# Sketched attention feeding a gated FFN: q by head in sixteen 32x32 tiles, numerators in column tiles, W without masks, wo in 2 KB rows, three products on GpSimd

## The chip, the cores and the metric

The kernel runs on one core of one Trainium2 chip. The metric is the device time of one execution in microseconds (us). The engines are TensorE (PE; its weight loads are listed apart as PEld), VectorE (DVE), ScalarE (ACT), GpSimd (POOL) and SyncE (SP), which here only issues transfers. Each engine works through its own queue in order.

## The reference, cut to what matters

There are 4 batches, 4 heads, 1088 tokens and 32 dimensions a head; the sketch rank r is 8. Then x, with 4352 rows of 128, goes through a gated FFN with 1536 hidden units.

```python
def phi(x):                       # 32 -> 64 features
    a = np.einsum('rd,bhsd->bhsr', S1, x)
    b = np.einsum('rd,bhsd->bhsr', S2, x)
    return np.einsum('bhsi,bhsj->bhsij', a, b).reshape(*x.shape[:-1], r * r)
q_p, k_p = phi(q), phi(k)
kv = np.einsum('bhsf,bhsd->bhfd', k_p, v)
z = np.sum(k_p, axis=2)
num = np.einsum('bhsf,bhfd->bhsd', q_p, kv)
den = np.einsum('bhsf,bhf->bhs', q_p, z)[..., None] + 1e-06
x = (num / den).transpose(0, 2, 1, 3).reshape(B * S, H * D)
out = (np.maximum(x @ w_gate, 0.0) * (x @ w_val)) @ w_out
```

## The kernel before, in words

The whole kernel is a list of tasks, each with an engine, an assumed cost, what it depends on and how many PSUM banks it needs. `Plan.run` (lines 86 to 198) turns the list into one static order: for each engine it takes, among the tasks that can start soonest, the one with the earliest due time (`due`, lines 57 to 84 for attention, `T0 + STEP * u` for FFN unit `u`). `find` (lines 100 to 119) gives a task its banks among seven of the eight; the eighth (`OB`) collects outputs. While attention tasks remain, FFN tasks may hold five banks (`f_max`) and attention three (`a_max`). The table `land` holds the times at which loads are assumed to land, and `at` keeps a task from being planned earlier. The order is fixed at build time; on the chip the engines wait for each other by semaphores.

**Keys** (lines 445 to 596), once per batch: k is loaded with head and 32 token groups on partitions and transposed in 32x32 blocks on DVE (`t1`, L453). Sixteen fp32 PE instructions (L465) multiply it with the masked sketch `sk` into two banks; DVE transposes the result back (`t2`, L482). `phi` (L344) makes the 64 features a token, `kv` (L574) sums features times v, `z` (L527) sums the features through the two sketches, `zd` (L538) masks z on DVE, `w` (L546) turns it into the vector W by which q gives the denominator, and `wst` (L554, DVE) stores W beside S1 and S2. `kvc` (L590, DVE) stores kv as a masked block diagonal.

**Queries** (lines 605 to 790) come in groups of 64-token blocks of two halves, so a group of n holds n x 128 tokens: batch 0 in groups of 1, 1, 2 and 4, batches 1 to 3 in groups of 8, and a last group of 2 for the remaining tokens of all batches. q stands with two heads and 64 tokens on partitions. `t1` (L651, L653, L656) transposes it on DVE, `ab` (L675, L680 for the last group) multiplies with S1, S2 and W of the batch in 64x64 tiles into two banks, with the weights of a head masked to its half; `t2` (L690) transposes back. `bw`, `dn`, `rd`, `an` (L700 to L717) make the denominator and divide the first sketch by it, and `phi` (L344) makes the features on POOL (on DVE for the first two groups). The features are transposed on PE (L734) or by DMA (L764, batches 1 to 3), `num` (L741) multiplies four blocks with kv in two full-width matmuls that accumulate, and ACT writes the result into `xT` (L783).

**FFN** (lines 793 to 901): 102 units of 512 products a partition. A unit is a gate matmul and a value matmul (L821) of 512 columns in all, each into its own bank; relu on ACT (L833); the product on DVE straight from PSUM (L842), after which the value bank is free; and four output matmuls (L853). A unit covers four blocks of 128 tokens for one slice of 128 hidden units (later groups) or one or two blocks for four or two slices (first groups).

**Loads**: SP loads S1, k and q of batch 0; POOL loads v of batch 0 with a cast (L275), then gate and value weights in three parts each, then wo (L409). `e_later` (L426) waits for the first weights to land by a small transfer that reads them (L427), then issues k of batch 1, waits for that in the same way (L429), then q and v of batch 1 and k and q of batch 2. The other loads come where the plan puts them on SP, as do the stores (L877, two a part of a group).

Filler matmuls on zeros (L917) are put into gaps of PE that the plan foresees before the first gate matmul: one for each 107 ns of a gap before `T_WARM`, one for each 57 ns of nine tenths of it later.

## Time and profile before

| | us |
|---|---|
| three executions | 105.01, 105.17, 106.96 (median 105.17) |
| the profiled execution | 105.96 |
| its span, first to last instruction | 104.0 |
| first gate matmul | 15.24 |
| q of batch 1 landed (first transpose of it) | 23.77 |
| first xT of batch 1 | 38.82 |
| last output copied out of PSUM | 100.46 to 100.75 |

The engine line gives busy time, share of the span and number of instructions. The slices cut the span in 40 parts of 2.6 us, with a digit for the busy tenths of each. A group line gives line, engine, operation, tiles and shapes, then the busy time, the mean ns of one, the idle time ahead, and what ended it. Means of matmuls are latencies of pipelined instructions; their cost in a dense stretch is read from the spacing of their starts.

### The profile page before, as it was taken

The page shows a single profiled execution, that of the slowest core. Times are in us where ns is not written, and L with a number is a line of the kernel's source. Part 1 is how long each engine was busy: PE and PEld are TensorE (multiplying, and loading weights), DVE is VectorE, ACT ScalarE, POOL GpSimd, SP SyncE. Part 2 cuts the span into 40 slices and gives each one's busy share as a digit, 9 for nine tenths or more (in the row PEclk, how much of TensorE's full clock was granted, in tenths as well). Part 3 has the DMA queues.
Part 4 walks back from the last instruction along what each step waited for, and adds up shares of the span by engine and source line. Part 5 has one row for each costly group of instructions (what it writes and reads, how often), then busy time and mean ns, then how long its engine had stood idle before and what let it go on. Part 6 is the DMA issues. An engine that isn't in the chain of part 4 may idle for free.

```text
span 104.0 us, 3090 instructions
## 1 busy us (share of the span) xinstructions
PE 98.2 (94%) x1166; PEld 66.5 (64%) x1166; DVE 91.2 (88%) x200; ACT 77.5 (74%) x156; POOL 48.4 (47%) x71
## 2 busy tenths in 40 slices
PE   5999999996999999999999999999999999999960
PEld 5847988785666655565575565655765666667950
DVE  2866677988999999999999999999997999899950
ACT  4457028869798838689997895899789969999930
POOL 6999716089929829530980970129700015000000
PEclk9999999999999999999999999999999999999997
DMA  1999899789402489997049104000673300130024
GB/s 18 292 225 169 183 217 116 239 209 324 144 2 54 83 145 129 298 338 181 3 87 199 23 0 104 0 0 0 59 176 75 92 18 0 26 75 0 6 48 106
DMA packets 15711, 11.60 MB, mean 111 GB/s; under 512 B 9040, under 2 KB 13392, under 8 KB 15696
## 3 DMA queue, kind: packets, MB, share of 16 engines
q1 hardware_dynamic: 12520, 9.87, 38.9%
q0 software_dynamic: 2992, 1.46, 10.8%
q8 instruction: 9, 0.15, 0.5%
q10 hardware_dynamic: 184, 0.07, 0.2%
q14 instruction: 6, 0.05, 0.2%
HBM read 9.05 MB, written 2.23 MB: 108 GB/s over the span
## 4 chain that ended last, share of the span: by engine, by line
PE 66%; DMA 16%; ACT 5%; POOL 4%; DVE 2%; SPq 1%; issue 1%; ACTq 0%; POOLq 0%
PE ps L821 37%; PE ps L853 19%; DMA q_sb<-in_q_dram 6%; DMA k_sb<-in_k_dram 5%; DMA wg<-in_moe_w_gate_dram 4%; ACT g_sb L833 3%; PE ps L675 3%; PE ps L741 3%; POOL v_sb L275 2%; PE ps L574 2%; PE ps L465 1%; DVE qt L653 1%; ACT xT L783 1%; SPq L427 1%; DVE ht L842 1%
## 5 line engine op out<-in xcount | busy, mean ns | idle before, releaser
L842 DVE TENSOR_TENSOR ht<-g_sb,ps 128x512 f16<-128x512 f16 x102 | 64.0, 674 | 2.9 <-ACT g_sb L833 2.2
L833 ACT ACTIVATE g_sb<-ps 128x512 f16<-128x512 f32 x102 | 58.2, 605 | 11.1 <-PE ps L821 8.6
L853 PEld LDWEIGHTS <-ht 128*128 128x128 f16 x408 | 29.3, 98 | 18.5 <-DVE ht L842 4.5
L853 PE MATMUL ps<-wo,ht 128*128 128x128 f16 x408 | 37.6, 219 | 0.9 <-ACT g_sb L833 0.9
L821 PE MATMUL ps<-xT,wv 128*128 128x512 f16 (+2 forms) x132 | 37.8, 331 | 0.0
L821 PE MATMUL ps<-xT,wg 128*128 128x512 f16 (+2 forms) x132 | 35.8, 330 | 0.3
L344 POOL TENSOR_TENSOR kp<-abk 128x512 f16<-128x512 f32 (+1 forms) x14 | 16.3, 1199 | 5.2 <-DVE abk L482 5.2
L344 POOL TENSOR_TENSOR qp<-an,abq 128x512 f16<-128x512 f32 x16 | 16.7, 1068 | 0.5
L821 PEld LDWEIGHTS <-wg 128*128 128x128 f16 x132 | 12.0, 97 | 3.6 <-issue 1.1
L700 POOL TENSOR_TENSOR bw<-abq 128x128 f32<-128x128 f32 (+1 forms) x9 | 3.8, 422 | 21.1 <-DVE abq L690 19.3
L821 PEld LDWEIGHTS <-wv 128*128 128x128 f16 x132 | 11.6, 98 | 2.6 <-issue 0.6
L917 PE MATMUL ps<-zero 128*128 128x128 f16 x75 | 8.8, 293 | 1.1 <-DVE maskkv L319 1.1
L717 POOL TENSOR_TENSOR an<-abq,rd 128x256 f32<-128x256 f32 (+2 forms) x6 | 2.9, 479 | 11.6 <-DVE rd L714 11.6
L917 PEld LDWEIGHTS <-zero 128*128 128x128 f16 x75 | 6.8, 134 | 1.4 <-DVE maskkv L319 1.1
L690 DVE STREAM_TRANSPOSE abq<-ps 128x512 f32<-128x512 f32 (+2 forms) x11 | 6.3, 583 | 0.6 <-PE ps L675 0.6
L783 ACT CAST xT<-ps 128x512 f16<-128x512 f32 (+2 forms) x11 | 5.4, 491 | 1.8 <-PE ps L741 1.7
L775 ACT COPY pt<-ps 128x256 f16<-128x256 f16 (+2 forms) x5 | 2.9, 584 | 4.7 <-PE ps L734 4.7
L870 ACT ACTIVATE o_st<-ps 128x512 f32<-128x512 f32 (+2 forms) x10 | 5.1, 515 | 0.9 <-PE ps L853 0.9
L453 DVE STREAM_TRANSPOSE kt<-k_sb 128x576 f32<-128x576 f32 (+1 forms) x8 | 5.5, 720 | 0.2 <-DMA k_sb<-in_k_dram 0.2
L675 PE MATMUL ps<-qt,wst 64*64 64x256 f32 (+3 forms) x112 | 5.5, 336 | 0.0
L741 PE MATMUL ps<-pt,kv_bd 128*128 128x512 f16 (+2 forms) x20 | 5.1, 336 | 0.0
L653 DVE STREAM_TRANSPOSE qt<-q_sb 128x512 f32<-128x512 f32 x6 | 4.1, 696 | 0.8 <-DMA q_sb<-in_q_dram 0.8
(76 smaller groups left out, 67.8 us busy)
## 6 DMA issues: line engine op xcount, KB each, us to landing
out_dram<-o_st SPq DMA_DIRECT2D x14, 128.0 KB, 2.5
k_sb<-in_k_dram SPq DMA_DIRECT2D x3, 544.0 KB, 4.2
q_sb<-in_q_dram SPq DMA_DIRECT2D x3, 544.0 KB, 5.9
v<-in_v_dram SPq DMA_DIRECT2D x9, 144.0 KB, 4.7
q_sb<-in_q_dram SPq DMA_DIRECT2D x3, 128.0 KB, 3.4
wg<-in_moe_w_gate_dram POOLq DMA_DIRECT2D x3, 128.0 KB, 4.8
wv<-in_moe_w_val_dram POOLq DMA_DIRECT2D x3, 128.0 KB, 4.9
wo<-in_moe_w_out_dram POOLq DMA_DIRECT2D x1, 384.0 KB, 7.3
```

What stands on the lines that cost most here:

```text
L344: eng.tensor_tensor(out=dst.rearrange("s x (i j) -> s x i j", i=R), in0=a[:, :, :, None].to_broadcast([128, n, R, R]), in1=b[:, :, None, : ...
L453: nc.vector.transpose(kt[b][:, lo:hi].rearrange("p c t -> p (c t)"), k_sb[b][:, lo * D:hi * D])
L653: nc.vector.transpose(G.qt[:, hp], src[:, hp, :, G.c0:G.c0 + G.n])
L675: nc.tensor.matmul(o, wst[G.bs[0]][r, hp].rearrange("p a f -> p (a f)"), G.qt[r, hp, st], start=True, stop=True, skip_group_check=True)
L690: nc.vector.transpose(G.ab[:, lo:hi].rearrange("p x h f -> p h x f"), ps[:, f.bank:f.bank + 2, lo * 32:hi * 32].rearrange("p h (x t) -> p ...
L741: nc.tensor.matmul(o, kv_bd[G.bs[0]][:, 2 * hp:2 * hp + 2].rearrange("f a d -> f (a d)"), G.ptc[:, hp, c0:c0 + n], start=hp == 0, stop=hp ...
L783: emit=lambda t, p=p, f=num: nc.scalar.copy(out=xT[:, p.col:p.col + p.n * 128], in_=ps[:, f.bank, 0:p.n * 128]))
L821: nc.tensor.matmul(ps[:, t.bank, y * W:(y + 1) * W], w[:, j], xT[:, p.col:p.col + W], start=True, stop=True)
L833: nc.scalar.activation(out=U.g_sb, in_=ps[:, g.bank], func=ACTF.Relu)
L842: nc.vector.tensor_tensor(out=U.ht, in0=U.g_sb, in1=ps[:, vv.bank], op=ALU.mult)
L853: nc.tensor.matmul(ps[:, ob() + s, 0:DM] if final else ps[:, OB, s * DM:(s + 1) * DM], U.ht[:, y * n * 128 + s * 128:y * n * 128 + (s + 1) ...
L917: nc.tensor.matmul(ps[:, OB, 0:128], zero, zero, start=True, stop=True)
```

## The change

- **q**: loaded like k, with head and 32 token groups on partitions. `ab` becomes sixteen matmuls, four heads by four token groups, each in a 32x32 tile, a head to a bank, so that it needs four neighbouring banks; the transpose back gives two banks free at a time. Batch 0 has two sketches (four blocks each) instead of four. The last group reuses the transposes of the others, so its own four go.
- **Numerators**: two heads to a 64-column tile, each with its own result rows, no accumulation and no zeros.
- **W**: `zd` and `wst` become plain copies on ACT, for the masks are not needed; S1 by head comes from one DVE transpose instead of a matmul with a selection. `kvc` moves to ACT for batches 1 to 3.
- **v of batch 0** is loaded by SP without a cast and cast on ACT. k and q have two buffers instead of four. Fills go to POOL, ahead of the weight loads.
- **Hidden units** are dealt so that wo comes in rows of 2 KB; the gate and value weights are then read with a step of four elements.
- **Units 1, 3 and 5** copy the value out of PSUM on ACT and multiply on POOL.
- **Stores** are one transfer a part. `NG` and `NH` grow from 10 and 14 to 12 and 16; `T_WARM` is 8000 instead of 5500, `STEP` 800 instead of 830, and some landing times differ.
- **Plan**: a task of four banks may exceed the attention limit by two, and while one waits, bank tasks that are due later are held back. Tasks on POOL keep to due times also after the first FFN unit.

```diff
+            most = self.n_banks
+            if t.kind == "f" and n_att:
+                most = self.f_max
+            elif t.kind != "f" and started_f:
+                most = self.a_max + 2 * (t.banks > 2)
...
+                    if started_f and t.banks and t.due > want:
+                        continue
...
-    load_q0(nc.sync, 0)
-    load_q0(nc.sync, 1)
+    load_q(nc.sync, 0, 0, 4 * Q0)
+    load_v(nc.sync, 0)
+    load_q(nc.sync, 0, 4 * Q0, KC)
...
+        nc.scalar.copy(out=wst[:, :, 0:2 * R],
+                       in_=ps[:, t_st.bank, None, 0:2 * R].to_broadcast([128, B, 2 * R]))
...
+        return w.rearrange("m (y f j) -> m y j f", y=3, j=JT)
...
+                emit=e_load(wo, moe_w_out.rearrange("(y f j) m -> f y (j m)", y=3, j=JT)))
...
+        K.zd = P.add(f"k{b}zd", "ACT", **act(32), deps=[x], emit=lambda t, b=b, z=K.z:
+                     nc.scalar.copy(out=zd[b], in_=ps[:, z.bank, 0:H * R]))
...
+            for h in range(H):
+                nc.tensor.matmul(ps[32 * h:32 * h + 32, z.bank, 64:64 + R], s1h[:, h],
+                                 zd[b][:, h * R:(h + 1) * R], start=True, stop=True)
...
+        def qe_ab(t, bs, c0, n):
+            for h in range(H):
+                r = slice(32 * h, 32 * h + 32)
+                for g in range(4):
...
+                    nc.tensor.matmul(
+                        ps[32 * g:32 * g + 32, t.bank + h, 0:n * 32], wst[r, b],
+                        qt[b][r, lo:lo + n].rearrange("p c t -> p (c t)"), start=True, stop=True,
+                        skip_group_check=True)
...
             for hp in range(2):
-                    nc.tensor.matmul(
-                        o, kv_bd[G.bs[0]][:, 2 * hp:2 * hp + 2].rearrange("f a d -> f (a d)"),
-                        G.ptc[:, hp, c0:c0 + n], start=hp == 0, stop=hp == 1)
+                o = ps[64 * hp:64 * hp + 64, t.bank, 0:n * 128]
+                for x, b in enumerate(G.bs):
+                    y = 128 // len(G.bs)
+                    nc.tensor.matmul(
+                        o.rearrange("f (c t) -> f c t", c=n)[:, :, x * y:(x + 1) * y], kv_bd[b][:, hp],
+                        G.ptc[:, hp, c0:c0 + n, x * y:(x + 1) * y], start=True, stop=True,
+                        skip_group_check=True)
...
+            def e_multp(t, U):
+                U.ht = f_h.tile([128, 512], FP16, name="ht")
+                nc.gpsimd.tensor_tensor(out=U.ht, in0=U.g_sb, in1=U.v_sb, op=ALU.mult)
+
+            on_pool = u in ON_POOL
...
-                n = int(max(gap - 100.0, 0.0) / 107.0) if now > 2000.0 else int(gap / 107.0)
+                n = int(max(gap + (0.0 if now < 2000.0 else 60.0), 0.0) / 107.0)
```

## The prediction, made before the changed kernel ran

> **What bounds the kernel now.** I read the page's engine line and slices first, then the windows view, then the groups of the long stretch, then the timeline of PE.
>
> ```profile
> PE 98.2 (94%) x1166; PEld 66.5 (64%) x1166; DVE 91.2 (88%) x200; ACT 77.5 (74%) x156; POOL 48.4 (47%) x71
> ...
> PE   5999999996999999999999999999999999999960
> ...
> DVE  2866677988999999999999999999997999899950
> ACT  4457028869798838689997895899789969999930
> ```
>
> PE and VectorE (DVE) both stand at nine tenths from the ninth slice on, so neither alone is the limit. The windows view puts numbers to it (columns: us, then busy us and count of PE, weight loads, DVE, ACT, POOL).
>
> ```profile
> 23.00:26.00 3.00, 2.11 (x29) 1.66 (x28) 2.23 (x5) 2.56 (x5) 3.00 (x4) 1.00 0.93 302
> 26.00:98.30 72.30, 72.06 (x785) 45.43 (x783) 70.15 (x131) 61.28 (x114) 30.04 (x34) 1.00 0.38 83
> ```
>
> DVE is busy 70.15 of 72.30 us. PE's 72.06 is a modelled figure, so I count its real work from the same stretch by the spacing of starts, not by the mean durations:
>
> ```profile
> L853 PE MATMUL ps<-wo,ht 128*128 128x128 f16 x350 | 33.3, 219 | 0.0
> L821 PE MATMUL ps<-xT,wv 128*128 128x512 f16 x84 | 31.0, 379 | 0.0
> L741 PE MATMUL ps<-pt,kv_bd 128*128 128x512 f16 x14 | 4.2, 379 | 0.0
> L675 PE MATMUL ps<-qt,wst 64*64 64x256 f32 x48 | 3.3, 389 | 0.0
> L680 PE MATMUL ps<-qt,wst 64*64 64x32 f32 x32 | 0.7, 223 | 0.0
> ```
>
> ```profile
> 37.97 0.38 PE L821 MATMUL ps<-xT,wv 128*128 128x512 f16 x1
> 38.19 0.59 PE L741 MATMUL ps<-pt,kv_bd 128*128 128x512 f16 x2
> 38.62 0.39 PE L853 MATMUL ps<-wo,ht 128*128 128x128 f16 x4
> ...
> 42.40 0.39 PE L853 MATMUL ps<-wo,ht 128*128 128x128 f16 x4
> 42.62 0.38 PE L821 MATMUL ps<-xT,wv 128*128 128x512 f16 x1
> 42.93 1.09 PE L675 MATMUL ps<-qt,wst 64*64 64x256 f32 x16
> 43.96 0.39 PE L821 MATMUL ps<-xT,wg 128*128 128x512 f16 x1
> ```
>
> Starts: a 128x512 takes 0.216 us (42.40 to 42.62 is four 128x128, 0.22; 38.19 to 38.62 is two 128x512, 0.43). So 350 x 0.056 = 19.6; 168 wide gate and value matmuls 36.3; 31 of 256 columns 3.4; numerators 14 x 0.216 = 3.0; the q sketch 48 in 3 x 1.03 = 3.1; the rest of attention about 5. Sum 70.4 of 72.3. PE and DVE are within one per cent of each other: a gain must come off both. Of the stretch before 26 us, the 23 to 26 window shows a hole (PE 2.11 of 3.00, DVE 2.23) where DVE stands 0.8 us behind the load of q for batch 1.
>
> **The change part by part.**
>
> *q sketch in sixteen tiles.* Per wide group 16 PE instructions become 32 (16 matmuls, fp32, two instructions each), each in a 32x32 tile. The 64x64 form takes 1.03 us from 42.93 to 43.96. Estimate from below: 16 x 256 columns over 4 tiles took 1.03; 32 over 16 tiles is half the columns for each tile, 0.5. From above: issue. L680's 32 instructions of 32 columns took 0.63 us (the chain: 83.78 to 84.41), 20 ns each, whatever their size; 32 of them 0.64, and with a tail 0.75. I take 0.64, because issue is the nearer row. Three groups: 3 x -0.39 = -1.2 (bounds -1.6 to -0.8). The last group (L680) stays at 32, nothing.
>
> *Numerators in column tiles.* Two 128x512 matmuls that accumulate (0.43 us) become two 64-column tiles that can stream side by side. That tiles do so is seen in L465: 16 instructions of 288 columns in 0.65 us, 41 ns each, where 288 columns alone are 121 ns (0.216 x 288/512). A change of tile form costs 0.09 us here: 42.62 to 42.93 is 0.31 where 0.216 is usual. So 0.216 + 0.09 = 0.31, at worst 0.43 + 0.09 = 0.52. I take 0.31, since L465's tiles do overlap: seven wide numerators, 7 x -0.12 = -0.8 (bounds -0.8 to +0.6). The Trainium skill, TensorEngine Tiling (Array Packing), Tiling Modes and Restrictions, says that a change of tiling mode drains the array and that column tiling gives up the fast weight load. The trace agrees on the drain (0.09 us); no row shows the second. [...]
>
> *DVE.* Off it go three products to GpSimd (L842, 64.0/102 = 0.63 each, -1.9, all before 26 us), four zd and four wst (0.18 and 0.17, -1.4), three kvc (0.28, -0.85), the four small q transposes of the last group (0.21, -0.85). One transpose of S1 comes (+0.2); the q transposes keep their elements. Total -4.8, of which 2.4 lies after 26 us: 70.15 becomes 67.8, enough to follow PE to 70.3 and no more slack than before (96%).
>
> *ACT* takes what DVE sheds: three copies of v (0.6), zd and wst (8 x 0.2), kvc (6 x 0.2), the cast of v0 (2 x 0.72); its fills (about 4 us, before 10 us) go. After 26 us 61.3 + 2.0 = 63.3 of 70.3, 90%: covered, but at 17 to 26 us 7.0 busy of 9 becomes about 9. If that cover goes, relu is late and PE waits for banks.
>
> *POOL* gets three products (128x512, nearest row L344 at 1.07 us: +3.2) in front of the products for batch 1 (kp at 23.61, 4.57 us). It had 3.6 us idle from 17 to 26, so they fit if q0's groups come no later. The third stands right ahead of kp of batch 1, worth +1.0 if POOL is late; but one kp now follows bw instead of preceding it, which gives 1.07 back.
>
> *Queues.* SP takes v of batch 0 (4 issues, 0.47 to 0.81 each by the rows of v) ahead of the second part of q0; POOL no longer issues it (2.37 us), so wg leaves up to 2 us earlier less the new memsets (eight of about 0.2). Then comes the gate that starts k and q of batch 1. Stores go from two issues to one. wo comes in fewer rows. The strided weights: 132 + 132 loads now step 8 bytes; L527's fp32 loads already step 8 bytes and take 112 to 121 ns against 104 to 112 for contiguous L465, so nothing; they hide behind 0.216 us matmuls, and only the 48 matmuls of 128 columns would show it (doubled, +2.6).
>
> *Start.*
>
> ```profile
> 12.97 1.07 PE L917 MATMUL ps<-zero 128*128 128x128 f16 x9
> 13.88 0.28 PE L734 MATMUL ps<-ident,qp 128*128 128x128 f16 x2
> ...
> 15.24 0.27 PE L821 MATMUL ps<-xT,wg 128*128 128x128 f16 x2
> ```
>
> The first gate matmul comes at 15.24, behind filler matmuls on zeros that come 0.10 us apart up to 13.88 (9 from 12.97) and 0.06 apart later (8 weight loads in 0.49). The first q sketch now covers four blocks: 32 instructions instead of 16 before the first transpose out, at the early pace of 28 ns (48 in 1.37) +0.4; z no longer stands behind L373, -0.4. The zd and wst copies now queue on ACT between the two casts of v0: if v0 lands at 9.2 (SP issue done by about 4.5 to 5.8, row of v 4.7 to landing), wst ends about where it did (9.87); if at 10.5, 1.5 us later. After kv, 22 fillers replace 9: at 0.10 they end at about 13.9 as now, at 0.06 about 1 us earlier. I take 0, bounds -1.0 to +1.5.
>
> *The hole at 23 to 26 us.* PE lost 0.89 us there. DVE, which is late, is rid of 1.9 us just before, and q of batch 1 can leave earlier: -0.9 (bounds -0.9 to 0, if q lands as late as now at 23.74).
>
> *Four banks at once.* A q sketch now needs four neighbouring PSUM banks of seven, and gives two back only after its first transpose (0.70 us, L690), the rest after the second. That is about 0.64 + 0.2 + 0.70 = 1.5 us with three banks for gate and value instead of five. PE would run 2.3 units of 0.65 us, 4.7 banks; with three it does 1.5, so it stands up to 0.5 us, or 1.0 with the time to clear the banks, unless finished products wait for L853 (0.22 us each; the pool of them grows to 16). The trace before shows no such wait, so between 0 and 1.0 for each of four groups (the second of batch 0 and the three wide ones). The compiled order puts up to four output units in front of such a sketch, so I take 0.1 each: +0.4 (bounds 0 to +4).
>
> *Tail.* After the last output 100.4 us the two last stores; the same transfer. 0.
>
> Sum: -1.2 - 0.8 + 0 - 0.9 + 0.4 = -2.5. Span 104.0 - 2.5 = 101.5. The profiled execution took 105.96 (1.96 around its span), 0.8 over the median 105.17. From the median: 105.17 - 2.5 = 102.7.
>
> **The rivals.**
>
> A second engine keeps the time. DVE falls from 70.15 to 67.8, POOL and ACT take more, and ACT is the one that frees gate banks. If orders on ACT (copies of v, casts, kvc, all in one queue with relu) make relu late by as much as PE gains, only a fifth stays: 105.17 - 0.5 = 104.7. For: ACT's 9 in the slices at 17 to 26 us. Against: after 26 us its 9.7 us of idle ahead of relu.
>
> Numerators gain nothing in column tiles: they stay serial with a change of form, 0.52 instead of 0.43, 7 x 0.09 = +0.6 in place of -0.8: 102.7 + 1.4 = 104.1. For: the 0.31 at each change of form. Against: L465. [...]
>
> The start is late: v0 lands at 10.5 behind q on SP, wst waits in ACT's queue behind its cast: +1.5, 104.2. For: v's 4.7 us. Against: it shares with 0.3 MB less of q than now.
>
> Slower: the four banks. At 0.7 us for each of four groups (+2.8 instead of +0.4) the gain is gone, 105.1; at 1.0, and with the sketch for the rest of all batches as a fifth, +5 instead of +0.4: 107.3. It decides from about 0.7 a group. For: DVE is full, so a transpose that frees banks also holds up the products that free others. Against: L853 gives PE 19.6 us of work that needs no new bank, and the two-bank sketch at 42.93 is followed at 43.96 with no gap.
>
> Better: the early clock rises (fillers 0.06 us apart from about 8 us), start -1.0 and sketches at their lower bound -0.4: 101.3.
>
> **How the numbers follow.** Forecast 0.48 (102.7, its own range 101.7 to 103.6; 0.38 of it below 103.07), better 0.10, second engine 0.10, numerators 0.08, late start 0.07, banks 0.17 (0.09 beyond 107.27). What a measurement of this kernel can tell from no change is about 2%: 103.07 to 107.27. Faster 0.38 + 0.10 = 0.48; same 0.10 + 0.10 + 0.08 + 0.07 + 0.08 = 0.43; slower 0.09. The range 101.0 to 106.0 leaves out part of the better case and the far end of the banks, near 0.2 together.
>
> **What would show it.** The wide sketch: 32 instructions in 0.64 us, start to next start. Wide numerators: 0.31 from start to next start. The products of units 1, 3 and 5 on POOL near 1.07, kp of batch 1 starting no later than 24.6. PE in the 3 us before its first 512-wide unit: over 2.8 busy. DVE near 86.4 in all, ACT after 26 us near 63. PE idle beside each sketch under 0.2. First gate matmul between 14.2 and 15.5. The prediction is wrong if PE stands over 0.7 us around each sketch waiting for relu or ht, if weight loads of wg and wv take much over 100 ns and show in the early 128-wide units, or if xT of batch 1 (now 38.82) comes later, since the 24 units of batch 0 end near it.

## The result, and the profile after

The changed kernel took 109.42 us (median of 4 runs, 108.96 to 109.84) against 105.11 for the kernel before: a ratio of 1.0412, with an interval of 1.0343 to 1.0481. The forecast was 102.7 with a range of 101.0 to 106.0. The change is 4.3 us slower instead of 2.5 faster. Medians here take in all executions of a kernel, ratios and their intervals only those that lie close to its fastest, so that a ratio can stand nearer to 1 than the medians do (e4 and e8).

The engine line and the slices of the changed kernel (a slice is now 2.7 us):

```profile
PE 95.9 (89%) x1244; PEld 65.8 (61%) x1244; DVE 87.6 (81%) x174; ACT 78.0 (72%) x161; POOL 49.1 (45%) x73
...
PE   6992999997999999999999979999999999999300
...
DVE  4573848859799999999999889999879898999300
ACT  4214039889788849599998757998899799999200
...
PEclk9999679999999999999999999999999999999965
```

The totals of the two fullest engines moved the way the forecast said: PE is busy 2.3 us less, DVE 3.6 less. Yet the span is 108.0 instead of 104.0. Three places in the slices are new. The last three PE digits read 300, where before they read 960 in smaller slices: the kernel now spends longer on something that is no engine's work. The fourth PE digit is a 2, and right behind it the granted clock falls to 0.6 and 0.7. And single 7s stand in the middle of the row. I split the span at the first gate matmul and at the last output matmul, and that gives the accounts (us):

| | before | after | difference |
|---|---|---|---|
| span's start to first gate matmul | 15.24 | 15.69 | +0.45 |
| first gate to last output matmul | 84.96 | 85.07 | +0.11 |
| last output matmul to span's end | 3.80 | 7.24 | +3.44 |
| span | 104.0 | 108.0 | +4.0 |

**The end** carries most of it. The first answer below is the DMA view of the kernel before in its last 5 us (40 slices of 0.125 us; the row gives the busy tenths of the 16 DMA engines, the lines under it the issues, with KB and median us to landing), the second that of the changed kernel in its last 9 us (slices of 0.225 us).

```profile
DMA  0000000000000038899659796699810200000000
...
out_dram<-o_st SPq DMA_DIRECT2D x2, 128.0 KB, 2.4
...
out_dram<-o_end SPq DMA_DIRECT2D x1, 64.0 KB, 2.2
```

```profile
DMA  0000000000026032112268954222221100000010
...
out_dram<-o_st SPq DMA_DIRECT2D x1, 256.0 KB
out_dram<-o_end SPq DMA_DIRECT2D x1, 64.0 KB, 5.1
```

The two last stores of 128 KB ran before at eight and nine tenths of the DMA engines. The one store of 256 KB that replaces them stands at two tenths for most of its time. By the packets of the trace, its 128 rows of 2 KB lie between 101.45 and 105.83, with 3.8 of 16 engines busy on average; before, the same 128 rows lay between 100.83 and 102.34, with 12.6 busy. The small store behind it on SP's queue lands 5.1 us after its issue instead of 2.2. SyncE then waits 4.1 us for the store at the end of the program, where it waited 0.4 before. From the view of its waits, the kernel before first:

```profile
SPq L947 <- DMA out_dram<-o_st: 0.4, 1, 0.4
...
SPq L935 <- DMA out_dram<-o_st: 4.1, 1, 4.1
```

**The start.** PE's timeline of the changed kernel before the first gate matmul (start, us, what; in brackets the idle time and what ended it), then ACT's at the same time:

```profile
10.49 0.51 PE L638 MATMUL ps<-qt,wst 32*32 32x128 f32 x32 [2.10 <-ACT wst L524]
...
11.76 2.54 PE L905 MATMUL ps<-zero 128*128 128x128 f16 x22
14.08 0.42 PE L710 MATMUL ps<-ident,qp 128*128 128x128 f16 x2
```

```profile
9.69 0.67 ACT L528 CAST v_sb<-v 128x576 f16<-128x576 f32 x1 [2.11 <-DMA v<-in_v_dram]
10.27 0.17 ACT L524 ACTIVATE wst<-ps 128x8 f32<-128x8 f32 x1
```

wst stands behind the first cast of v on ACT, v lands at 9.69, and so the first sketch comes at 10.49 after 2.10 us of idle PE. The windows view then shows what the idle time does (columns as in the prediction; the granted clock is the last number but two). By the trace's clock record the clock was full from 4.56 on, earlier than in the kernel before (13.84); the new fillers do that (e10 below). From there the record changes only at steps of 3.41 us, and I cut the windows at these steps:

```profile
4.56:7.97 3.41, 3.21 (x65) 1.95 (x63) 2.66 (x7) 0.87 (x6) 1.87 (x3) 1.00 1.09 238
7.97:11.39 3.42, 1.32 (x52) 0.94 (x53) 1.24 (x3) 1.31 (x3) 3.16 (x5) 1.00 1.14 304
```

```profile
11.40:14.80 3.40, 3.40 (x42) 3.40 (x38) 3.04 (x16) 0.26 (x1) 0.31 (x1) 0.50 1.12 198
```

PE was busy 1.32 us in the second step, and in the third the clock is 0.50. The 22 fillers of that step, planned for 0.057 us each, start 0.107 us apart. What the fillers won, the wait gave back. The Trainium skill, TensorE: Matmul & The Clock Gate, Part 1, speaks of a free-running window of about 3.4 us after which the clock is set; the trace agrees with the length. It names an idle window as what halves the clock; here 1.32 us of work did not prevent it.

**The long stretch** is even at +0.11, but not because nothing happened. I summed PE's time from each start to the next, by kind, and took waits as what exceeds the usual spacing. Waits rose from 1.44 us (1.05 at 24.55, 0.26, 0.13) to 3.35 in ten pieces (0.59 at 25.8, 0.47 at 56.2 and 0.85 at 63.0 the largest), +1.9. So the work itself fell by 1.8: the three wide sketches from 3.08 to 1.95, the last group's from 0.64 to 0.33, the wide numerators from 3.03 to 2.37; changes of tile form, which now come more often, take a part of that back. Here is the largest of the waits, in PE's timeline:

```profile
62.86 0.39 PE L839 MATMUL ps<-wo,ht 128*128 128x128 f16 x4
63.93 0.73 PE L638 MATMUL ps<-qt,wst 32*32 32x256 f32 x32 [0.69 <-DVE ht L809]
64.59 0.41 PE L788 MATMUL ps<-xT,wv 128*128 128x512 f16 x1
```

A sketch of four banks waits for a product of DVE to leave the fourth. (The bracket says 0.69, because it counts from the modelled end of the matmul before; from start to start the wait is 0.85.)

### The profile page after: what moved, and what is told of

It is laid out like the page before. It is cut to its first block, busy times and chain, and to the rows that moved or that the text cites. A ratio compares the mean times of both kernels' runs of the same rounds, so it can differ in the third digit from the quotient of the medians.

```text
span 108.0 us, 3211 instructions
## 1 busy us (share of the span) xinstructions
PE 95.9 (89%) x1244; PEld 65.8 (61%) x1244; DVE 87.6 (81%) x174; ACT 78.0 (72%) x161; POOL 49.1 (45%) x73
## 4 chain that ended last, share of the span: by engine, by line
PE 74%; ACT 7%; DMA 5%; SPq 3%; issue 2%; DVE 2%; ACTq 0%
PE ps L788 40%; PE ps L839 20%; DMA v<-in_v_dram 5%; ACT g_sb L800 4%; PE ps L905 3%; PE ps L638 3%; PE ps L717 3%; PE ps L441 2%; DVE ht L809 2%; PE ps L535 1%; SPq L283 1%; PE ps L503 1%; ACT v_sb L528 1%; SPq L273 1%; ACT pt L742 1%
## 5 line engine op out<-in xcount | busy, mean ns | idle before, releaser
L809 DVE TENSOR_TENSOR ht<-g_sb,ps 128x512 f16<-128x512 f16 x99 | 62.2, 674 | 5.7 <-ACT g_sb L800 4.4
L788 PE MATMUL ps<-xT,wg 128*128 128x512 f16 (+2 forms) x132 | 35.0, 331 | 0.4 <-ACT g_sb L800 0.3
L788 PEld LDWEIGHTS <-wv 128*128 128x128 f16 x132 | 13.2, 114 | 5.0 <-issue 3.0
L788 PEld LDWEIGHTS <-wg 128*128 128x128 f16 x132 | 13.5, 115 | 2.4 <-issue 0.4
L905 PE MATMUL ps<-zero 128*128 128x128 f16 x91 | 9.6, 277 | 1.0 <-DVE maskt L317 1.0
L905 PEld LDWEIGHTS <-zero 128*128 128x128 f16 x91 | 8.0, 130 | 1.8 <-DVE maskt L317 1.0
L528 ACT CAST v_sb<-v 128x576 f16<-128x576 f32 x8 | 5.4, 698 | 2.1 <-DMA v<-in_v_dram 2.1
L638 PE MATMUL ps<-qt,wst 32*32 32x256 f32 (+2 forms) x192 | 3.6, 324 | 2.8 <-ACT wst L524 2.1
L626 DVE STREAM_TRANSPOSE qt<-q_sb 128x544 f32<-128x544 f32 (+2 forms) x8 | 5.8, 732 | 0.1
```

Source lines behind the costliest of these rows:

```text
L528: deps=[l_late.get(f"v{b}")], emit=lambda t, b=b, x=x: nc.scalar.copy(out=v_sb[b][:, 2 * x:2 * x + 2], in_=v32[b % 2][:, 2 * x:2 * x + 2]))
L626: nc.vector.transpose(qt[b][:, lo:hi].rearrange("p c t -> p (c t)"), q_sb[b][:, lo * D:hi * D])
L638: nc.tensor.matmul(ps[32 * g:32 * g + 32, t.bank + h, 0:n * 32], wst[r, b], qt[b][r, lo:lo + n].rearrange("p c t -> p (c t)"), start=True, ...
L788: nc.tensor.matmul(ps[:, t.bank, y * W:(y + 1) * W], hidden(w)[:, j // JT, j % JT], xT[:, p.col:p.col + W], start=True, stop=True)
L809: nc.vector.tensor_tensor(out=U.ht, in0=U.g_sb, in1=ps[:, vv.bank], op=ALU.mult)
L905: nc.tensor.matmul(ps[:, OB, 0:128], zero, zero, start=True, stop=True)
```

## The experiments

Each was timed beside the kernel before, whose median was 104.67 to 104.76. "First gate", "stretch" (first gate to last output matmul) and "end" (last output matmul to span's end) are read from the profiled execution of each.

**e1: four transfers a store.** The changed kernel; each part is stored in four transfers of 32 rows of partitions instead of one.

```diff
-            nc.sync.dma_start(out=x, in_=o_sb[:, 0:p.n])
+            for g in range(4):
+                nc.sync.dma_start(out=x[g], in_=o_sb[32 * g:32 * g + 32, 0:p.n])
```

> The changed kernel with each store issued as four transfers, one for each 32-partition token group, instead of one whose outermost loop has four steps. Theory A (the loss is at the end: the last store of 256 KB moves on about four of sixteen DMA engines, 3.8 busy on average from 101.45 to 105.83, where before 12.6 were busy): the four spread like those of before. Three more issues of 0.5 us stand ahead of the last one, so the span falls from 108.0 to about 105.2, the time by about 2.8 to 106.6. Theory B (the loss is inside: waits for four banks and the late start): the end of PE stays near 101.0 and the time falls by less than 1 us, since the transfer is as large as it was.

Measured: 106.03 us (105.83 to 106.92), ratio 1.0164 [1.0079, 1.0249]; 3.4 us less than the changed kernel. First gate 14.96, stretch 85.08, end 3.96. The DMA view of its last 5 us:

```profile
DMA  0000000000089344915976998168200000000000
...
out_dram<-o_st SPq DMA_DIRECT2D x4, 64.0 KB, 1.8
```

The stretch is that of the changed kernel to 0.01 us, and the end is that of the kernel before to 0.2. The store lasts from 100.36 to 102.27 with 9.1 engines busy, although SP spends 1.73 us on issuing four. The single store was the 3.4 us, more than the 2.8 that had been expected.

Its start shows a second thing. PE idles 2.05 us before the first sketch, as in the changed kernel, and the clock stays full. The windows view at the steps of its own clock, which rose at 6.29:

```profile
6.29:9.70 3.41, 2.36 (x54) 1.64 (x46) 2.63 (x5) 0.49 (x2) 2.47 (x2) 1.00 1.17 254
9.70:13.11 3.41, 2.20 (x72) 2.00 (x73) 1.51 (x11) 1.31 (x3) 1.89 (x4) 1.00 1.09 275
```

Here the same idle spell is parted between two steps, each with over 2 us of work. Whether the late v also costs the clock depends on where the steps fall in an execution. With full clock all along, the changed kernel's start reaches the first gate at 14.96 here and at 14.73 in e7; the kernel before's start, in the executions of e2 and e10 that had full clock all along, at 13.58 and 13.57. Clock against clock the change starts 1.2 to 1.4 us late; the 15.24 of the kernel before's own profile hid it, because that execution had the half clock until 13.84.

**e2: the kernel before with one store.** Its two transfers of 64 rows become one with an outer loop of two.

```diff
-            for st in range(2):
-                c = CA * st + G.c0 + p.c0
-                nc.sync.dma_start(out=x[:, c:c + p.n], in_=o_sb[64 * st:64 * st + 64, 0:p.n])
+            c = G.c0 + p.c0
+            y = x[:, c:c + p.n]
+            y = bass.AP(tensor=y.tensor, offset=y.offset, ap=[[CA * DM, 2], [C * DM, T], [1, p.n * DM]])
+            nc.sync.dma_start(out=y, in_=o_sb[:, 0:p.n].rearrange("p c m -> p (c m)"))
```

> The kernel before with only its stores merged: one transfer of 256 KB whose outermost loop has two steps (of 64 rows), instead of two transfers of 64 rows. Theory A: about two engines busy, 128 rows of 2 KB at 0.13 us each over two engines are 8.3 us instead of 1.5, so the span grows from 104.0 by 6 us or a little more, PE's end unchanged near 100.4. Rival (the store is slow because one transfer is twice as large): the last store takes 3 to 4 us instead of 2.4, +1 us.

Measured: 108.95 us (108.77 to 109.12), ratio 1.0428 [1.0339, 1.0516]: this one edit makes the kernel before as slow as the changed one. The DMA view of its last 9.5 us (slices of 0.24 us):

```profile
DMA  0000001110113133694111111111111111000000
...
out_dram<-o_st SPq DMA_DIRECT2D x1, 256.0 KB
```

One tenth of the engines for most of the time: 2.0 busy, from 99.04 to 105.34, 6.3 us (8.3 had been expected, from 0.13 us a row; a row took 0.10). An outer loop of two runs on two engines, one of four on 3.8 (the changed kernel), 64 rows on 12.6 (the kernel before). Bytes, rows and row length are the same in all three, so it is not the size; and it is not the single issue, for the two single issues differ, and SP's small store of 64 KB, one issue too but with 128 rows outermost, has its packets between 102.27 and 102.62 in e1 with 10.0 engines busy. What goes with the engines is the count of the outermost loop. The Trainium skill, DMA: Bandwidth & Descriptors, Why a DMA increments its semaphore by 16 and not by 1, states it: a transfer uses the largest number of engines up to 16 that divides the slowest dimension of both sides. The traces agree on 2 and 4.

**e3: W ahead of the casts of v.** The changed kernel with the casts of v of batch 0 behind wst on ACT.

```diff
-                      deps=[l_late.get(f"v{b}")], emit=lambda t, b=b, x=x: nc.scalar.copy(
+                      deps=[l_late.get(f"v{b}")], after=[K.wst] if b == 0 else (),
+                      emit=lambda t, b=b, x=x: nc.scalar.copy(
```

> The changed kernel with wst of batch 0 ahead of both casts of v of batch 0 in ACT's queue, stores as they are. Theory A1 (the late start is carried to the end): wst moves from 10.27 to about 8.2, the first q sketch from 10.49 to about 8.5, PE keeps its fast clock, the first gate matmul falls from 15.69 to 14.2 to 14.7, and the time by 1.0 to 1.4 us. Theory B1 (batch 1 is the next limit: its first xT at 38.98 ends the wait for FFN work of batch 0): the first gate is as early, but the gate matmul after 39 us moves by less than 0.3 us, and the time by less than 0.4.

Measured: 109.28 us (108.48 to 110.92), ratio 1.0433 [1.0315, 1.0551]. PE's timeline:

```profile
8.41 0.50 PE L639 MATMUL ps<-qt,wst 32*32 32x128 f32 x32
...
10.72 0.19 PE L536 MATMUL ps<-v_sb,kp 128*128 128x64 f16 x1 [1.37 <-ACT v_sb L529]
11.29 0.77 PE L536 MATMUL ps<-v_sb,kp 128*128 128x64 f16 x17 [0.38 <-ACT v_sb L529]
...
15.62 0.55 PE L789 MATMUL ps<-xT,wg 128*128 128x128 f16 x7
```

The sketch came 2.1 us earlier, as the edit meant, and the first gate at 15.62 instead of 15.69. PE's wait only moved to kv, which needs the same cast of v; in the clock step from 8.26 to 11.68 PE was busy 1.67 us, and the clock was halved from 11.68 to 15.09. In this execution the order on ACT gained nothing, for the clock was halved either way; so the early start that was expected (14.2 to 14.7) did not come, and e3 cannot say what one is worth. e4 and e9 can.

**e4: e1 and e3 together.**

> Both edits of the two kernels above on the changed kernel. Theory A with A1: the two gains add, about 4 us less than the changed kernel, about 105.4, near before. With B1 instead: only the store's, about 106.4. Theory B: above 108.

Measured: 106.4 us (104.93 to 107.69, 10 runs), ratio 1.0099 [1.0035, 1.0164]. In the profiled execution (105.15 us) the clock stayed full from 4.15 on (the waits for v are 0.45 and 0.38 us here), the first gate came at 13.55, and the stretch grew to 85.84, with waits of 0.76 us for wo, which landed at 17.70, and 0.88 for an output copy at 24.2. The ten times fall into two groups, 104.9 to 105.2 and 106.4 to 107.7. That they are executions without and with the drop of the clock fits the mean granted clock, which is on record for each: 0.994 to 1.0 in the four of the lower group, 0.970 to 0.980 in five of the six above. The sixth, 106.45 us, has 1.0 and is not explained.

**e5: v of batch 0 loaded and cast by POOL as before,** on top of e1 (the cut shows the load and the cast; the plan's figures for them go back too).

```diff
-    load_v(nc.sync, 0)
...
+    prev = l_v0 = P.add("ld_v0", "POOL", 2000, 2000, emit=lambda t: load_v(nc.gpsimd, 0))
...
+        K.v = [l_v0] if b == 0 else [P.add(f"v{b}{x}", "ACT", **act(2 * CA * D), at=land.get(f"v{b}", 0.0),
```

> The changed kernel with four transfers a store (its profile: first gate matmul 14.96, last output matmul 100.04) and with v of batch 0 loaded and cast by POOL's queue as in the kernel before, so that ACT casts nothing for batch 0. Theory S (the late start comes from v of batch 0: it lands at 9.69 through SP and holds wst, kv and PE behind it): with the clock fast from about 6 us the first gate matmul comes at 13.6 to 14.1, as in the kernel before with a fast clock (13.58), and the end of PE moves by as much, to about 99. Rival (only the moment at which PE's clock becomes fast sets the start): the first gate at a fast clock stays within 0.3 of 14.96.

Measured: 106.33 us (106.07 to 107.98), ratio 1.016 [1.0085, 1.0235]. The first gate comes at 13.16, 1.8 us earlier than in e1 with full clock in both, and the stretch is 86.38, 1.3 longer: wo lands at 17.85 and PE waits 1.17 us for it, then 0.88 at 24.3. So v of batch 0 was what made the start late, as the theory said. But the end of PE moved by 0.5 us only, to 99.54 instead of the expected 99: most of the early start is lost again within ten microseconds.

**e6: no products on POOL,** on top of e1.

```diff
-    ON_POOL = (1, 3, 5)
+    ON_POOL = ()
```

> The changed kernel with four transfers a store, and no unit's product on GpSimd: units 1, 3 and 5 multiply on DVE again (+1.9 us there before 26 us, three copies of 0.6 us less on ACT). Theory I1 (the gain inside is lost where PE waits for banks and for ACT): the stretch from the first gate matmul to the last output matmul, 85.1 us, changes by less than 0.5 us. Rival (DVE is what limits the stretch before 26 us): it grows by 1 us or more.

Measured: 105.35 us (104.68 to 106.26, 10 runs), ratio 1.0068 [1.0019, 1.0117]. The first gate comes at 15.52, with the clock halved from 10.21 to 13.62. Against the changed kernel, which starts its stretch at nearly the same time (15.69), the stretch falls from 85.07 to 84.39, although PE's waits for banks are still there, now at other sketches. PE's timeline at the first wide sketch of batch 2:

```profile
41.81 0.39 PE L839 MATMUL ps<-wo,ht 128*128 128x128 f16 x4
42.72 0.73 PE L638 MATMUL ps<-qt,wst 32*32 32x256 f32 x32 [0.52 <-ACT g_sb L800]
```

This sketch is released by a relu on ACT, the one of the changed kernel at 63.93 by a product on DVE. The first xT of batch 1 comes at 38.03 instead of 38.98, and from there to the last output matmul it takes 61.88 us instead of 61.78. So the products on POOL cost the time ahead of that xT, where the forecast had given them a gain for DVE; both expectations (less than 0.5 us of change, or 1 us more) missed. The mechanism is read below from POOL's timeline.

**e7: without the rule that holds later tasks back while one waits for four banks,** on top of e1.

```diff
-                    if started_f and t.banks and t.due > want:
-                        continue
```

> The changed kernel with four transfers a store, its plan without the rule that holds back later bank tasks while a sketch of four banks waits. Theory I1 (the waits come from collecting four neighbouring banks): the order changes there, the wait of 0.85 us at 62.3 ahead of the sketch of batch 3 moves or grows and the stretch from first gate to last output matmul, 85.1 us, changes by 0.5 to 3 us, upwards if the rule was a help. Rival (the waits are for something else, such as relu being late): the stretch stays within 0.3.

Measured: 106.75 us, ratio 1.0203 [1.014, 1.0267]; the stretch is 85.73, 0.65 longer than in e1, with waits of 0.97 and 0.86 us near 78, one for transposed features and one for xT. In these profiles the order without the rule is the worse one; the times of the two kernels overlap (106.35 to 106.92 against 105.83 to 106.92).

**e8: the kernel before with numerators in 64-column tiles,** nothing else.

```diff
-                        o, kv_bd[G.bs[0]][:, 2 * hp:2 * hp + 2].rearrange("f a d -> f (a d)"),
-                        G.ptc[:, hp, c0:c0 + n], start=hp == 0, stop=hp == 1)
+                        ps[64 * hp:64 * hp + 64, t.bank, 0:n * 128], kv_bd[G.bs[0]][:, 3 * hp],
+                        G.ptc[:, hp, c0:c0 + n], start=True, stop=True, skip_group_check=True)
```

> The kernel before with its numerators of batches 0 to 3 in two 64-column tiles, nothing else changed (the static order too). Theory N (work taken off PE alone is not time, for DVE is as full): the pair takes 0.33 instead of 0.43 us, -0.7 us of PE work in all, but the stretch from the first gate to the last output matmul, 84.8 to 85.0 us, shrinks by less than 0.4. Rival (PE alone sets the pace): it shrinks by 0.6 to 0.7 us.

Measured: 105.16 us (103.73 to 106.06, 10 runs), ratio 1.0012 [0.9955, 1.0068]: no difference, but the interval would also hold half of the 0.7 us at stake, so the trace has to say it. In the profile the fourteen matmuls fall from 3.03 to 2.38 us from start to start, and the changes of form ahead of them add about 0.6 (seven of 0.09). From xT of batch 1 to the last output it takes 61.41 us against 61.38. The stretch is 0.58 shorter, more than the theory's 0.4, but all of that lies ahead of xT of batch 1: the wait at 24.55 is 0.13 in place of 1.05, and one of 0.40 for an output copy comes at 30.5. DVE takes up q of batch 1 at 22.92 with no wait for the load, where it waited 0.80 us for it until 23.77; the tiles have no part in that.

**e9: e6 with W ahead of the casts of v** (the edit of e3).

> The changed kernel with four transfers a store, no products on GpSimd, and wst of batch 0 ahead of the casts of v of batch 0 on ACT. Theory L1 (an early start is lost again before 39 us, because batch 1's first xT comes when its own chain lets it): the first gate matmul comes at about 13.5 with a fast clock, but batch 1's first xT stays within 0.5 of 38.03 and the time within 0.5 of 105.35. Rival (the products on GpSimd and wo behind them were what ate the early start): batch 1's first xT comes near 36.5, and the time falls to about 104.

Measured: 105.1 us (104.14 to 106.04, 10 runs), ratio 1.0029 [0.998, 1.0077]. This time the clock stayed full from 5.49 on. PE's timeline:

```profile
8.47 0.50 PE L639 MATMUL ps<-qt,wst 32*32 32x128 f32 x32
...
10.02 0.19 PE L536 MATMUL ps<-v_sb,kp 128*128 128x64 f16 x1 [0.61 <-ACT v_sb L529]
...
13.67 0.61 PE L789 MATMUL ps<-xT,wg 128*128 128x128 f16 x8
```

The idle time ahead of kv was 0.61 and 0.38 us instead of 1.37 and 0.38 in e3, PE was busy 2.42 us in the clock step that holds it, and the clock did not fall. The first gate came 1.85 earlier than in e6's profile, the stretch was 0.64 longer (85.03), and the medians are 0.25 apart. The theory missed here: it held the first xT of batch 1 to 38.03 within 0.5, and it came at 36.84, where the rival had 36.5; the 104 us that the rival expected came in the fastest execution (104.14), not in the median. It is the best of the kernels that keep the change's form, and cannot be told from the kernel before.

**e10: the kernel before with the changed kernel's fillers,** nothing else of the change.

```diff
-    T0, STEP, T_GATE, T_DT, T_WARM, SLACK = 12500.0, 830.0, 11000.0, 1700.0, 5500.0, 500.0
-    P = Plan(free={"PE": 1200.0, "ACT": 3100.0, "DVE": 3600.0, "POOL": 3000.0, "SP": 5000.0},
+    T0, STEP, T_GATE, T_DT, T_WARM, SLACK = 12500.0, 830.0, 11000.0, 1700.0, 8000.0, 500.0
+    P = Plan(free={"PE": 1060.0, "ACT": 3100.0, "DVE": 3600.0, "POOL": 3000.0, "SP": 5000.0},
...
-                n = int(max(gap - 100.0, 0.0) / 107.0) if now > 2000.0 else int(gap / 107.0)
+                n = int(max(gap + (0.0 if now < 2000.0 else 60.0), 0.0) / 107.0)
```

> The kernel before with the fillers of the changed one alone: their number counted as there, up to 8 us of the plan at the slow pace. Theory C (what sets the first gate matmul of the kernel before is when PE's clock becomes fast: 13.84 us in its own profile with the first gate at 15.24, 5.82 us with 13.58 in the run of its merged stores): the clock is fast from about 4.5 to 7 us in every execution, the first gate near 13.6, and the median falls by about 1 us to 103.7, the best executions staying where they are. Rival (the early fast clock only came by chance and is lost at the next idle spell): median within 0.4 of the kernel before.

Measured: 104.3 us (103.69 to 105.11, 9 runs), ratio 0.9966 [0.9931, 1.0001]. Full clock from 6.12, first gate at 13.57, stretch 84.81. It has the lowest median of all kernels here, 0.4 us below the kernel before, and its interval just reaches 1. Its profile starts 1.7 us earlier than that of the kernel before, and the median gains 0.4, not the 1 us that was expected; the rival had said within 0.4, so the times do not part the two. The profiles do: in all eleven kernels with these fillers the clock was full from 3.9 to 6.8 us on, in the three with the old ones from 5.82 (e2), 13.80 (e8) and 13.84 (the kernel before itself). That the kernel before starts early in some executions anyhow would explain the small gain; its other executions were not profiled.

**e11: the three wide sketches in two halves of two banks,** on top of e6.

```diff
...
+            if turned:
+                abs2 = []
+                for hs in (range(0, 2), range(2, 4)):
+                    abs2.append(P.add(f"q{i}ab{hs[0]}", "PE", 450, 670, banks=2, after=abs2[:],
+                                      deps=t1 + free + [kk[b].wst for b in bs],
...
```

> The changed kernel with four transfers a store and no products on GpSimd, its three wide q sketches split into two tasks of two heads and two banks each. Theory I1 (PE waits to collect four neighbouring banks): the waits ahead of the sketches (0.45 at 25.8 and 0.69 at 42.0 without the products, 0.85 at 62.3 with them) go; the halves cost about 0.45 us each, +0.25 a batch; the stretch from first gate to last output, 84.4 us, falls by 0.3 to 1. Rival (banks are short whoever takes them): the waits reappear elsewhere and the stretch grows by the 0.7 us of PE work.

Measured: 106.63 us, ratio 1.0171 [1.0107, 1.0236]. No wait over 0.1 us is left ahead of the wide sketches, which fits waits for four banks (the order round them changed too). But the stretch is 84.83 against e6's 84.39, where a fall was expected: a half takes 0.59 us from its start to the next, not 0.45, so that two cost 1.19 where the whole sketch took 0.65.

**e12: hidden units in plain order,** on top of e6: weights contiguous, wo in rows of 512 bytes.

```diff
-        return w.rearrange("m (y f j) -> m y j f", y=3, j=JT)
+        return w.rearrange("m (y j f) -> m y j f", y=3, j=JT)
...
-                emit=e_load(wo, moe_w_out.rearrange("(y f j) m -> f y (j m)", y=3, j=JT)))
+                emit=e_load(wo.rearrange("f y (j m) -> f (y j) m", j=JT), moe_w_out.rearrange("(j f) m -> f j m", f=128)))
```

> The changed kernel with four transfers a store and no products on GpSimd, hidden units dealt as before: gate and value weights contiguous, wo in rows of 512 bytes. Theory W (the step of 8 bytes in the weights is hidden): weight loads fall from 114 to 97 ns, the stretch from first gate to last output, 84.4 us, stays within 0.3. Rival (the step shows): the stretch falls by 0.5 or more, most of it before 26 us where the matmuls have 128 columns.

Measured: 105.52 us (104.77 to 106.48, 9 runs), ratio 1.0058 [1.0021, 1.0095], against e6's 1.0068. The weight loads in its group view:

```profile
L788 PEld LDWEIGHTS <-wv 128*128 128x128 f16 x132 | 11.7, 98 | 4.9 <-issue 2.4
L788 PEld LDWEIGHTS <-wg 128*128 128x128 f16 x132 | 11.6, 98 | 2.7 <-issue 0.7
```

In the changed kernel they take 114 and 115 ns. The step of 8 bytes makes a load 16 to 17 ns longer, and that is hidden: the stretch differs by 0.18 (84.21 against 84.39).

## Why the prediction was wrong, step by step

**Tail: "the same transfer. 0." This step failed, and with it the forecast.** The change part had noted "Stores go from two issues to one" and priced it at nothing. The bytes are the same; the transfer is not. Its outermost loop has 4 steps instead of 64, and it ran on 3.8 engines instead of 12.6, which cost 3.4 of the 4.0 us of span. e1 takes the 3.4 us out of the changed kernel, e2 puts 4.2 into the kernel before. No bound was given for this step and no rival had it: the diff's list of transfers was counted by issues, and the last one, which nothing covers, was not looked at for its shape. The earlier stores of the same form hurt no one, since FFN work lies beside them: with and without them the stretch is 85.07 and 85.08 in the changed kernel and e1, 84.80 and 84.81 in e2 and e10.

Without it the change is worth +1.3 us (e1 at 106.03 against 104.76). That, too, is not the -2.5 of the sum. Where it lies shows when the profiles are split at the first xT of batch 1 (us; the last column runs to the start of the last output matmul, and "W first" is the edit of e3):

| | first gate | first xT of batch 1 | from there on |
|---|---|---|---|
| before | 15.24 | 38.82 | 61.38 |
| e10, before with full clock early | 13.57 | 37.01 | 61.37 |
| changed | 15.69 | 38.98 | 61.78 |
| e1, four transfers a store | 14.96 | 38.26 | 61.78 |
| e4, four transfers and W first | 13.55 | 37.61 | 61.78 |
| e6, four transfers, no POOL products | 15.52 | 38.03 | 61.88 |
| e9, four transfers, no POOL products, W first | 13.67 | 36.84 | 61.86 |

The last column hardly moves, whatever happens ahead of it: 61.4 in the kernel before, 61.8 to 61.9 in the changed form. There the forecast had about -1.2 (two wide sketches, five numerators, banks for two) and got +0.4. Ahead of it, e1 is 1.25 later than e10, both at full clock; W first and no products on POOL take more than that off together (e9). The steps one by one:

**Sketch in sixteen tiles: the number right, the reason not.** Predicted 32 instructions in 0.64 us for 1.03, as issue at 20 ns each, whatever their size. Measured in PE's timeline of the changed kernel, where the two groups that follow also show the numerators:

```profile
27.22 0.71 PE L638 MATMUL ps<-qt,wst 32*32 32x256 f32 x32
27.86 0.41 PE L788 MATMUL ps<-xT,wv 128*128 128x256 f16 x2
28.11 0.38 PE L788 MATMUL ps<-xT,wg 128*128 128x256 f16 x2
28.42 0.41 PE L717 MATMUL ps<-pt,kv_bd 128*64 128x512 f16 x2
28.76 0.40 PE L839 MATMUL ps<-wo,ht 128*128 128x128 f16 x4
```

27.22 to 27.86 is 0.64. But the last group has 32 instructions too, of 64 columns, and they take 0.33:

```profile
84.39 0.39 PE L638 MATMUL ps<-qt,wst 32*32 32x64 f32 x32
84.72 0.62 PE L788 MATMUL ps<-xT,wg 128*128 128x512 f16 x2
```

With 128 columns they take 0.43 (16.45 to 16.88), and in the trace most of them start 7 ns apart. So the time goes with the columns, and issue at 20 ns was not what bounded the wide sketch; that it gave the right size there is luck. The last group thus fell from 0.64 to 0.33 where nothing was expected.

**Numerators in column tiles: the term was mis-sized.** Predicted 0.31 for 0.43. The two tiles do run side by side: their starts lie 0.004 us apart in the trace, and 28.42 to 28.76 is 0.34, one matmul of 0.22 and 0.12 until the next form begins. Ahead of them 28.11 to 28.42 is 0.31 instead of 0.22, 0.09. So the pair costs 0.43 with its way in and out, as before. So the rival "Numerators gain nothing" was right in its title, not in its reason or price (it had them serial, 0.52), and in e8 the edit alone leaves the time from xT of batch 1 on as it was (61.41). The forecast had counted the change of form on one side of the pair only, 0.09, and the trace shows it on both, 0.09 and 0.12. The Trainium skill, TensorEngine Tiling (Array Packing), Tiling Modes, says that a change of tiling mode drains the array; the trace agrees with these two figures.

**Start: "I take 0", and the rival of a late v.** The profile's +0.45 is within the bounds of -1.0 to +1.5, but by accident of the clock (and 15.69 lies outside the 14.2 to 15.5 that were to show it). At full clock in both the difference is the 1.2 to 1.4 us of e1's section, near the rival's +1.5 and by its mechanism: v landed at 9.69, between the two cases given (9.2 and 10.5), and wst waited behind its cast. Putting wst ahead of the casts gives it back: first gate at 13.55 in e4, at full clock. But of these 1.4 us only 0.65 are left at the first xT of batch 1 (37.61 against e1's 38.26), for PE then waits for wo, 0.76 us until 17.70, and for an output copy, 0.88 until 25.08. With the products on POOL gone as well (e9, also at full clock) that xT comes at 36.84, within 0.2 of e10's 37.01; PE still waits 0.64 for wo there, but no longer for the output copy. It takes both edits. What the forecast had not seen is that a wait this early can halve the clock for 3.41 us more.

**The hole at 23 to 26 us: moved, not gone, and not always there.** The -0.9 was read from one execution of the kernel before. The wait that makes the hole, 1.05 us in its profile, is 0.13 in e8, 0.14 in e2 and 0.50 in e10, whose order and loads are the same up to there; DVE takes up q of batch 1 at 22.92, 21.89 and 21.96 in them instead of 23.77. In the changed kernel PE was busy 2.89 of those 3.00 us, as the step said (over 2.8). But 0.43 us were lost just behind it, waiting for an output copy on ACT at 26.46, and the next window has 3.53 of 4.00. xT of batch 1 came at 38.98 against 38.82. The prediction had named this as the test for being wrong: the units of batch 0 end there, so what PE wins earlier than that is worth nothing unless attention of batch 1 is early too. It was not. POOL's timeline of the changed kernel shows why:

```profile
18.00 1.18 POOL L817 TENSOR_TENSOR ht<-g_sb,v_sb 128x512 f16<-128x512 f16 x1 [1.34 <-ACT v_sb L813]
...
24.41 1.17 POOL L817 TENSOR_TENSOR ht<-g_sb,v_sb 128x512 f16<-128x512 f16 x1
25.53 3.55 POOL L336 TENSOR_TENSOR kp<-abk 128x512 f16<-128x512 f32 x3
```

The features of k of batch 1 start at 25.53 instead of 23.61 (the forecast allowed 24.6), for two reasons: the third product stands right ahead of them (1.12 us), and the features of batch 0's last q group ahead of it begin at 22.36 instead of 21.56, behind the second product, for which POOL sat idle 1.15 us until ACT's copy came. In e6, without the products, they start at 23.89, and the stretch is shorter by 0.7 us.

**Four banks: +0.4 was too little.** Waits in the long stretch rose by 1.9 us, where the forecast had +0.4 for banks and -0.9 for the hole. Some are for banks (e11 removes those ahead of sketches), some for relu and output copies on ACT. The rival "slower: the four banks" had the mechanism, and at 0.85 us the largest of these waits passes its 0.7, but at one group of four only; it does not decide alone.

**The rest.** DVE fell to 87.6 where 86.4 was forecast. The strided weights cost next to no time, as said (0.18 us of stretch in e12), though a load does take 16 to 17 ns longer, where the forecast had nothing. ACT's total rose only by 0.5 us.

What stays open: how the 1.9 us of additional waits in the long stretch divide between banks and ACT's lateness, since every edit that removed one kind also changed the order of the tasks. The one execution of e4 that took 106.45 us at a mean clock of 1.0 is not explained. A single store with its 32 rows outermost, which would keep one issue and many engines, was not tried.

## What to carry to other kernels

Of every transfer that a change merges or reshapes, read the outermost loop and not only bytes and issues, and first of the last one, which no work covers; the DMA row of the final microseconds shows it at once. A saving on the busiest engine counts only up to the next point where it waits for another chain, so find that point (here xT of batch 1 at 39 us) and ask what the change does to that chain. When two tile forms alternate, price the change of form on the way in and on the way out before counting what the tiles save.

## What the runs showed of the hardware that was not expected

- A store of 128 rows of 2 KB took 6.3 us with an outer loop of 2 (2.0 DMA engines busy), 4.4 with one of 4 (3.8), 1.9 as four transfers of 32 rows (9.1), and 1.5 as two of 64 rows (12.6). One issue is no bar by itself: 64 KB in 128 rows, one issue with the rows outermost, took 0.35 us with 10.0 engines busy (e1).
- Thirty-two fp32 instructions in sixteen 32x32 tiles took 0.33 us with 64 columns, 0.43 with 128 and 0.65 with 256; sixteen of them in eight tiles, 256 columns, still took 0.59 (e11).
- The granted clock changes only in steps of 3.41 us from where it first rose, and one step with little work sets the next to half: after 1.32 us of busy PE (changed kernel), 1.67 (e3), 2.06 (e6), 1.21 (e11) and 1.14 (e12). Steps with 2.20 (e1), 2.42 (e9) and 2.37 (e10) did not. One with 1.78 (e7) did not either, so busy time as the profile counts it does not give the limit exactly. The same idle spell of 2.1 us halves the clock or not by where the steps fall (changed kernel and e1).
- The same start had full clock from 5.82 in one profiled execution (e2) and from 13.84 in another (the kernel before), 1.66 us apart at the first gate matmul.
- A product of two fp16 operands into fp16 took GpSimd 1.17 us for 128x512, longer than the 1.07 of its fp32 products of the same size:

```profile
L336 POOL TENSOR_TENSOR qp<-an,abq 128x512 f16<-128x512 f32 x16 | 16.7, 1069 | 0.5
...
L817 POOL TENSOR_TENSOR ht<-g_sb,v_sb 128x512 f16<-128x512 f16 x3 | 3.5, 1170 | 2.5 <-ACT v_sb L813 2.5
```
